# Weight bits on three engines, a softmax in pieces, and a new instruction list, in one fused attention and feed-forward kernel

## The chip, the cores and the metric

The kernel runs on one core of a Trainium2 chip. The core has TensorE (PE in the rows), VectorE (DVE), ScalarE (ACT), GpSimd (POOL) and SyncE (SP), which here only issues DMA transfers. The metric is the device time of one execution in microseconds, from a median of runs.

## What is computed

For 8 batches and 8 heads of 576 rows with 64 columns, linear attention: a softmax of each row of q over its 64 columns, a softmax of each column of k over its 576 rows, a 64 by 64 product of k and v per head, and q times it. The result, 4608 rows of 512, goes through a feed-forward block:

```python
h = x @ w_in                                   # 512 -> 1024
e = np.exp(h - h.max(-1)); sm = e / (e.sum(-1) + 1e-9)
solu = h * sm
ln = (solu - mean(solu)) / sqrt(var(solu) + 1e-6) * g_ln
out = ln @ w_out                               # 1024 -> 512
```

q, k and v are 32-bit floats. The two weights arrive as 64-bit floats, which the kernel turns into 32-bit floats itself.

## The kernel before

The 4608 rows are cut into 36 row tiles of 128. Batches have four whole tiles (c = 0 to 3); the last 64 rows of two neighbouring batches share a fifth. The first four tiles, all of batch 0, are "whole" tiles: they use 32-bit matmuls with unscaled weights. All others use products of 16-bit high and low halves.

Every piece of work is a generator, and one `next` on it is a step. The order is written out by hand: `ORDER` is one string, whose words name the generator to step next, "Q0a.v" meaning that the steps' free operations go to VectorE (".v"), ScalarE (".a") or GpSimd (".p"). Each engine executes its instructions in the order in which the list issues them, so a late instruction holds up all behind it on its engine.

The names in the list: LQb, LKb, LG and the first steps of w, y and V issue loads. Qba, Qbb, Qbc are the softmaxes of q (Q0a and Q0b one whole tile each, Q0c two). Kb is the key side of batch b: the maximum of each column over rows (lines 372 to 377, VectorE), which goes through TensorE to be spread (turned, L348; col, L351; cols, L354; wide, L358; kb, L361), the subtraction (L383, GpSimd or VectorE), exp (L385, ScalarE), 144 small matmuls in two halves (L397), the division (kvn, L409), the largest entry (mx, L413; L172, L175) and from it a power of two s with which the 16-bit copies bd are made (L426 to L432). xt is the attention product of tile t: L561 and two copies xT for whole tiles (the projection after it takes both), L585 with high and low halves (L595, L597) for the others. ht is the first projection of tile t (L612 in four quarters of four matmuls for whole tiles, L620 for others) and the chain behind it (L627 to L676): maximum, exp, a few 128x1 operations for a power of two p, product, sum, high and low halves u, transposing DMA, sum of squares. ot is the second projection (L694) and its eviction. `h` in PSUM has two buffers, so ht starts when the tile two before has had its squares read (L663).

wi and yi (i = 0 to 3) bring 1024 columns' worth of 64-bit words of w_in and w_out into one of two buffers, and `float_of` (L251) makes 32-bit floats of them: ScalarE takes the high words through a scaled Prelu (L259), VectorE shifts the result left by 3 (L261) and ors the top 3 bits of the low words into it (L263). Then ScalarE sums the absolute values (L276, L313). W and Z find the largest sum, a power of two from it, and write the 16-bit high (L288, L335, ScalarE) and low parts (L290, L337, VectorE) of the weights. The 32-bit weights also serve L612 as they are.

P is a group of four matmuls on zeros whose result nobody reads (L751); the list has eight of these. V copies (L212) put v beside a column of ones, on ScalarE unless the list says otherwise.

Of the kernel before, what the change touches and what calls it, by code (L numbers as in the profile page):

```python
# [12 lines left out]
I32 = mybir.dt.int32  # L13
AF = mybir.ActivationFunctionType
# [86 lines left out]
def linear_attention_solu_ffn(ctx: ExitStack, tc: tile.TileContext, q, k, v, w_in, w_out, g_ln, out):  # L101
# [52 lines left out]
    def on(default):  # L154

        return chosen["engine"] or default

    def cast(eng, out, x):
        if eng is nc.scalar:
            eng.copy(out, x)  # L160
# [655 lines left out]
```

## Time and profile before

| | |
|---|---|
| median of 3 runs | 464.75 us (463.77 to 465.03) |
| the profiled execution's own time | 464.6 us |
| its span, first to last instruction | 462.8 us |
| PE busy | 439.2 us, 95% |
| DVE busy | 339.3 us, 73% |
| ACT busy | 285.2 us, 62% |
| POOL busy | 202.6 us, 44% |

The profiled execution lasted 1.8 us longer than its span, and 0.15 us less than the median. In a timeline row the first two numbers are start and duration in microseconds; an instruction that starts behind another on its engine can overlap it by some tenths. Brackets give the engine's idle time before the row and what ended it. A row with "xN" is N instructions in a row, taken together.

### The profile page before, as it was taken

The page shows a single profiled execution, that of the slowest core. Times are in us where ns is not written, and L with a number is a line of the kernel's source. Part 1 is how long each engine was busy: PE and PEld are TensorE (multiplying, and loading weights), DVE is VectorE, ACT ScalarE, POOL GpSimd, SP SyncE. Part 2 cuts the span into 40 slices and gives each one's busy share as a digit, 9 for nine tenths or more (in the row PEclk, how much of TensorE's full clock was granted, in tenths as well). Part 3 has the DMA queues.
Part 4 walks back from the last instruction along what each step waited for, and adds up shares of the span by engine and source line. Part 5 has one row for each costly group of instructions (what it writes and reads, how often), then busy time and mean ns, then how long its engine had stood idle before and what let it go on. Part 6 is the DMA issues. An engine that isn't in the chain of part 4 may idle for free.

```text
span 462.8 us, 8794 instructions
## 1 busy us (share of the span) xinstructions
PE 439.2 (95%) x3379; PEld 212.9 (46%) x3379; DVE 339.3 (73%) x622; ACT 285.2 (62%) x492; POOL 202.6 (44%) x308
## 2 busy tenths in 40 slices
PE   0688999999999999999999999999999999999997
PEld 0344444455445445444544445444454444444445
DVE  4989999987987979986987888675778553541711
ACT  2779998777767768385756674567635654441500
POOL 2112856487776664741455575126613421122010
PEclk9999999999999999999999999999999999999999
DMA  8897866788698496958697857774342562322252
GB/s 280 292 305 267 239 137 184 149 226 203 179 230 187 89 243 111 273 114 217 120 252 153 180 121 185 203 166 86 86 93 68 92 130 77 72 66 68 59 120 72
DMA packets 137386, 73.98 MB, mean 160 GB/s; under 512 B 114168, under 2 KB 122624, under 8 KB 137344
## 3 DMA queue, kind: packets, MB, share of 16 engines
q1 hardware_dynamic: 137344, 73.42, 65.1%
q8 instruction: 26, 0.43, 0.4%
q14 instruction: 16, 0.13, 0.1%
HBM read 36.70 MB, written 9.44 MB: 100 GB/s over the span
## 4 chain that ended last, share of the span: by engine, by line
PE 86%; ACT 7%; DVE 3%; DMA 1%; issue 1%; SPq 0%; ACTq 0%
PE o L694 41%; PE h L620 36%; PE kv L397 4%; PE x L585 3%; DMA km<-in_k_dram 1%; ACT gw L259 1%; ACT e L633 1%; PE h L612 1%; ACT km L385 1%; ACT wi L288 1%; ACT junk_out L313 1%; PE warm_up L751 1%; PE wide L358 1%; DVE iw L263 1%; ACT e L663 1%
## 5 line engine op out<-in xcount | busy, mean ns | idle before, releaser
L694 PE MATMUL o<-wo,uT 128*128 128x512 f16 (+1 forms) x888 | 197.8, 373 | 0.0
L620 PE MATMUL h<-wi,xT 128*128 128x512 f16 x768 | 178.0, 379 | 0.3 <-ACT e L663 0.3
L694 PEld LDWEIGHTS <-uT 128*128 128x128 f16 x888 | 85.8, 98 | 97.7 <-issue 1.6
L620 PEld LDWEIGHTS <-xT 128*128 128x128 f16 x768 | 74.3, 98 | 88.2 <-issue 1.8
L627 DVE TENSOR_REDUCE top<-h 128x1 f32<-128x1024 f32 x36 | 44.0, 1221 | 29.3 <-PE h L620 29.1
L656 DVE SCALAR_TENSOR_TENSOR u<-h,nmu,u 128x1024 f16<-128x1024 f32 x36 | 45.8, 1275 | 16.3 <-ACT u L654 16.1
L663 ACT ACTIVATE e<-h,nmu 128x1024 f32<-128x1024 f32 x36 | 40.1, 1113 | 21.2 <-DVE u L656 21.1
L649 DVE SCALAR_TENSOR_TENSOR h<-h,ph,e 128x1024 f32<-128x1024 f32 x36 | 46.1, 1283 | 8.1 <-POOL ph L646 6.1
L637 POOL TENSOR_SCALAR am<-nm 128x1 f32<-128x1 f32 x20 | 9.1, 454 | 80.7 <-ACT nm L629 80.6
L643 POOL TENSOR_TENSOR p<-pi,mone 128x1 f32<-128x1 f32 x36 | 25.5, 708 | 39.9 <-DVE pi L640 38.4
L654 ACT ACTIVATE u<-h,nmu 128x1024 f16<-128x1024 f32 x36 | 40.0, 1113 | 1.0
L633 ACT ACTIVATE e<-h,nm,hs 128x1024 f32<-128x1024 f32 x28 | 33.7, 1202 | 0.7
L704 ACT ACTIVATE os<-o,rr 128x512 f32<-128x512 f32 (+1 forms) x21 | 14.2, 674 | 30.2 <-PE o L694 22.9
L651 ACT ACTIVATE nmu<-s 128x1 f32<-128x1 f32 x36 | 7.3, 202 | 39.8 <-DVE h L649 31.9
L449 POOL TENSOR_TENSOR qm<-qm,qnmx 128x1024 f32<-128x1024 f32 (+1 forms) x12 | 21.1, 1770 | 20.6 <-DVE qnmx L447 20.5
L612 PE MATMUL h<-iw,xT 128*128 128x512 f32 x64 | 29.5, 599 | 0.1
L629 ACT ACTIVATE nm<-top,hs 128x1 f32<-128x1 f32 x28 | 8.2, 294 | 33.4 <-DVE top L627 33.4
L467 POOL TENSOR_TENSOR qm<-qm,qrec 128x1024 f32<-128x1024 f32 x12 | 23.0, 1920 | 11.7 <-DVE qrec L458 5.4
L383 POOL TENSOR_TENSOR km<-km,kb 128x1152 f32<-128x1152 f32 x10 | 26.3, 2632 | 3.4 <-ACT kb L361 3.2
L597 DVE SCALAR_TENSOR_TENSOR xT<-x,xT 128x512 f16<-128x512 f32 (+1 forms) x36 | 22.3, 623 | 7.2 <-ACT xT L595 7.1
L702 DVE TENSOR_SCALAR os<-o,rr 128x512 f32<-128x512 f32 (+1 forms) x16 | 11.6, 728 | 20.6 <-PE o L694 15.3
L474 POOL TENSOR_TENSOR qhl<-qm,qhl 128x512 f16<-128x512 f32 x20 | 24.1, 1228 | 5.3 <-ACT qhl L160 5.1
(147 smaller groups left out, 559.9 us busy)
## 6 DMA issues: line engine op xcount, KB each, us to landing
v<-in_v_dram SPq DMA_DIRECT2D x32, 288.0 KB, 3.9
km<-in_k_dram SPq DMA_DIRECT2D x7, 1152.0 KB, 6.4
out_dram<-os SPq DMA_DIRECT2D x31, 256.0 KB, 2.7
qm<-in_q_dram SPq DMA_DIRECT2D x7, 1024.0 KB, 6.7
w_in<-in_moe_w_in_dram SPq DMA_DIRECT2D x8, 512.0 KB, 8.4
w_out<-in_moe_w_out_dram SPq DMA_DIRECT2D x8, 512.0 KB, 5.8
out_dram<-os SPq DMA_DIRECT2D x10, 128.0 KB, 2.3
km<-in_k_dram SPq DMA_DIRECT2D x2, 576.0 KB, 6.8
```

Of the source, the lines that this page charges most:

```text
L383: on(nc.gpsimd).tensor_tensor(km[:, ns], km[:, ns], wide, op=ALU.subtract)
L474: on(nc.gpsimd).tensor_tensor(lo, y, hi, op=ALU.subtract)
L612: nc.tensor.matmul(h[:, ns], xT[:, kc], iw[kc][:, ns], start=(i == 0), stop=(i == NP - 1))
L620: nc.tensor.matmul(h[:, ns], xT[:, t, kc], wi[:, s, kc, ns], start=(i == 0), stop=(i == len(terms) - 1))
L627: nc.vector.tensor_reduce(top, h, axis=AX.X, op=ALU.max, negate=True)
L633: nc.scalar.activation(e, h, AF.Exp, bias=nm, scale=hs, accum_out=z)
L643: nc.gpsimd.tensor_tensor(p, pi, mone, op=ALU.pow)
L649: nc.vector.scalar_tensor_tensor(h, h, ph, e, op0=ALU.mult, op1=ALU.mult, accum_out=s1)
L654: nc.scalar.activation(u[:, 0], h, AF.Identity, bias=nmu)
L656: nc.vector.scalar_tensor_tensor(u[:, 1], h, nmu, u[:, 0], op0=ALU.add, op1=ALU.subtract)
L663: nc.scalar.activation(e, h, AF.Square, bias=nmu, accum_out=s2)
L694: nc.tensor.matmul(o, uT[:, j, f], wo[:, s, f, cols], start=(f == 0 and j == 0 and s == 0), stop=(f == NF - 1 and j == 1))
```

## The change

`float_of` takes the bits of the low words in a step of their own ahead of the Prelu, in place in the words' buffer: on GpSimd from the words' top byte (a multiplication and an addition on bytes, rounded to an integer), or on VectorE with a shift where the list says ".v". Left shift and or become one VectorE instruction. The v copies and the high parts of the weights go to ScalarE, or to GpSimd where the list says ".v". In the softmax of q of the four whole tiles, the subtraction, the single exp and the sum on VectorE give way to one exp per head and tile on ScalarE, with the negated maximum as bias and the sum as accumulator output: 8 in Q0a, 8 in Q0b, two steps of 8 in Q0c. `ORDER` is another list of the same steps, 1692 in both.

```diff
@@ v copies
-        cast(on(nc.scalar), vm[:, i, :, 0:D], t)
+        cast(scalar_or_pool(), vm[:, i, :, 0:D], t)
+    def scalar_or_pool():
+        return nc.gpsimd if on(nc.scalar) is nc.vector else nc.scalar
@@ float_of
+        eng = on(nc.gpsimd)
+        if eng is nc.vector:
+            eng.tensor_scalar(low, low, 29, -1, op0=ALU.logical_shift_right, op1=ALU.bitwise_and)
+        else:
+            top = words.bitcast(U8)[:, :, 3]
+            eng.tensor_scalar(low, top, 1.0 / 32, -31.0 / 64, op0=ALU.mult, op1=ALU.add)
+        yield
         nc.scalar.activation(x, high.bitcast(F32), AF.Prelu, scale=2.0**-112, alpha=-(2.0**32))
         yield
-        nc.vector.tensor_scalar(xi, xi, 3, -1, op0=ALU.logical_shift_left, op1=ALU.bitwise_and)
-        yield
-        nc.vector.scalar_tensor_tensor(xi, low, 29, xi, op0=ALU.logical_shift_right, op1=ALU.bitwise_or)
+        nc.vector.scalar_tensor_tensor(xi, xi, 3, low, op0=ALU.logical_shift_left, op1=ALU.bitwise_or)
         yield
@@ weights_in_scaled, weights_out_scaled
-            nc.scalar.activation(wi[:, 0, kc], iw[kc], AF.Copy, scale=s)
+            cast_scaled(scalar_or_pool(), wi[:, 0, kc], iw[kc], s)
-            nc.scalar.activation(wo[:, 0, f], x, AF.Copy, scale=g)
+            cast_scaled(scalar_or_pool(), wo[:, 0, f], x, g)
@@ q_softmax
-        on(nc.gpsimd).tensor_tensor(x, x, wide(nmx), op=ALU.add)
-        yield
-        nc.scalar.activation(x, x, AF.Exp)
-        yield
         sums = sm.tile([P, n], F32, name=f"qsum{name}", tag="qsum")
-        nc.vector.tensor_reduce(shaped(sums), x, axis=AX.X, op=ALU.add)
+        if places is not None:
+            cs = len(places)
+            for c in range(cs):
+                for hd in range(H):
+                    y = x[:, hd] if cs == 1 else x[:, hd, c]
+                    i = slice(hd * cs + c, hd * cs + c + 1)
+                    nc.scalar.activation(y, y, AF.Exp, bias=nmx[:, i], accum_out=sums[:, i])
+                yield
+        else:
...
@@ ORDER, the first words
-    "LQ0*2 LK0 Q0a*2 Q0c LK0 K0.v Q0c.v K0 w3 K0.v K0 Q0b Q0a.v w3 K0 V02 Q0a Q0b K0.v Q0a.v Q0c V00 K0.v "
-    "LG w3 K0.v V02 Q0b.v w0 LG w0 K0 V01 K0.v w3 V00 V03 Q0a w3 K0.v Q0a w2 P w0 w2 K0.v K0 K0.v V01 "
-    "K0.v w0 V03 w0 w3 K0.v P K0 LG w2 w1 Q0b.v Q0c.v K0 Q0b w2 Q0b.v w1 Q0b P K0 x0.v LK1 w0 K0 Q0c.v K0 "
...
+    "LQ0*2 LK0 LG Q0a LG Q0c Q0a Q0b K0 Q0b.v LK0 K0*2 K0.v P K0 Q0c.v V00 V00.v K0 w3 Q0a.v P Q0b.v K0.v "
+    "K0 Q0a w3 V02 Q0b.v w0 K0 P w3.v*2 K0.v Q0a.v w0 w3.v K0 K0.v Q0b.v V01.v Q0b V02.v LG P Q0a V03 w2 "
+    "V01.v K0.v*2 w0.v w0 K0*2 V03.v w2*2 w0.v Q0c K0 V10 K0.v w2.v Q0c*2 w1 w0 K0 x0 w1.v x0 x0.v LK1 "
...
```

In both lists eight P steps stand. In the list before, all eight come behind K0's first transposes on TensorE, three of them ahead of K1's: one before, one between and one behind the two halves of K0's small matmuls. In the new one two come ahead of K0's first transposes, one between these and the spreading ones, one ahead of K0's small matmuls, none between their halves, and four behind K1's first transposes. Of the eight "low" steps of w and y, those of w3 and w0 are on VectorE and six on GpSimd. Up to the step that starts x4, the v copies on ScalarE go from eight to two (V13, V12) and those on GpSimd from none to six; wi's third high part and four of wo's eight are on GpSimd.

## Rows read from the trace of the kernel before

**Rows 1.** The span in five stretches, cut at TensorE's first instruction, at the end of K1's first transposes, at the end of h3's last matmuls and at TensorE's last instruction: start:end and length, busy time and number of instructions of PE, PE's weight load, DVE, ACT and POOL, granted TensorE clock, DMA share, GB/s.

```profile
0.00:14.30 14.30, 0.01 (x1) 0.04 (x1) 8.00 (x20) 4.87 (x7) 3.78 (x9) 1.00 0.88 306
14.30:38.50 24.20, 21.05 (x230) 12.13 (x231) 21.55 (x43) 19.53 (x32) 2.09 (x2) 1.00 0.87 292
38.50:72.30 33.80, 31.28 (x265) 14.32 (x263) 32.50 (x59) 33.39 (x58) 19.97 (x21) 1.00 0.69 184
72.30:459.50 387.20, 386.90 (x2886) 186.41 (x2885) 277.28 (x503) 226.98 (x398) 176.73 (x276) 1.00 0.63 145
459.50:462.80 3.30, 0.00 (x0) 0.00 (x0) 0.00 (x0) 0.47 (x1) 0.00 (x0) 0.85 0.11 40
```

**Rows 2.** The timeline of TensorE from its first warm-up group to the end of h3.

```profile
17.23 1.91 PE L751 MATMUL warm_up<-bd 128*128 128x512 f16 x4
...
22.38 1.89 PE L751 MATMUL warm_up<-bd 128*128 128x512 f16 x4
24.19 1.58 PE L397 MATMUL kv<-vm,km 64*64 64x65 f32 x72
...
27.15 0.67 PE L561 MATMUL x<-qT,kvn 64*64 64x128 f32 x16
...
29.33 3.70 PE L612 MATMUL h<-iw,xT 128*128 128x512 f32 x8
32.87 0.60 PE L519 MATMUL qt<-ident,qn 128*128 128x128 f32 x4
...
38.17 0.38 PE L348 MATMUL turned<-ident,ktop 128*128 128x128 f32 x2
38.39 1.03 PE L751 MATMUL warm_up<-bd 128*128 128x512 f16 x4
...
70.27 1.98 PE L612 MATMUL h<-iw,xT 128*128 128x512 f32 x4
```

**Rows 3.** ScalarE's instructions by line and shape over the span: count, busy us and mean ns of one, idle time before.

```profile
L451 ACT ACTIVATE qm<-qm 128x1024 f32<-128x1024 f32 x15 | 15.8, 1051 | 1.8 <-DVE qm L449 1.4 <-POOL qm L449 0.4
L629 ACT ACTIVATE nm<-top,hs 128x1 f32<-128x1 f32 x28 | 8.2, 294 | 33.4 <-DVE top L627 33.4
L651 ACT ACTIVATE nmu<-s 128x1 f32<-128x1 f32 x36 | 7.3, 202 | 39.8 <-DVE h L649 31.9 <-DVE p_kv L182 5.5 <-DVE den L404 2.4
L259 ACT ACTIVATE iw<-w_in 128x1024 f32<-128x1024 f32 x4 | 4.6, 1140 | 1.7 <-DMA w_in<-in_moe_w_in_dram 1.7
L451 ACT ACTIVATE qm<-qm 128x512 f32<-128x512 f32 x2 | 1.3, 628 | 5.7 <-POOL qm L449 5.7
```

**Rows 4.** The timeline of ScalarE: K0's spreading, its second exp, and a sum of absolute values with the accumulator read behind it and the instruction that follows.

```profile
15.44 0.40 ACT L160 COPY cols<-col 128x256 f32<-128x256 f32 x1 [0.62 <-DVE col L351]
...
16.62 0.37 ACT L361 COPY kb<-wide 128x256 f32<-128x256 f32 x1 [0.20 <-PE wide L358]
...
20.61 1.17 ACT L385 ACTIVATE km<-km 128x1152 f32<-128x1152 f32 x1
...
32.75 1.06 ACT L276 ACTIVATE junk_in<-iw 128x1024 f32<-128x1024 f32 x1 [1.21 <-DVE iw L263]
33.71 0.19 ACT L276 ACTIVATION_READ_ACCUMULATOR junk_in<-iw 128x1 f32 x1
33.80 0.49 ACT L426 ACTIVATE bd<-kvn,s_kv 64x256 f16<-64x256 f32 x1
```

**Rows 5.** The timeline of VectorE: the first two maxima of q, the column maxima, the largest entry of kvn and the last word step of w_in.

```profile
6.12 1.81 DVE L447 TENSOR_REDUCE qnmx<-qm 128x8 f32<-128x512 f32 x2 [5.12 <-DMA qm<-in_q_dram]
...
14.98 0.42 DVE L351 TENSOR_REDUCE col<-turned 128x4 f32<-128x256 f32 x1 [0.24 <-PE turned L348]
...
28.01 0.41 DVE L413 TENSOR_REDUCE mx<-kvn 128x1 f32<-128x256 f32 x1
...
31.43 1.23 DVE L263 SCALAR_TENSOR_TENSOR iw<-w_in,iw 128x1024 int32<-128x1024 int32 x1
```

**Rows 6.** VectorE's and then GpSimd's instructions in the same form.

```profile
L383 DVE TENSOR_TENSOR km<-km,kb 128x1152 f32<-128x1152 f32 x6 | 8.0, 1351 | 0.7 <-ACT kb L361 0.7
L261 DVE TENSOR_SCALAR gw<-gw 128x1024 int32<-128x1024 int32 x4 | 2.7, 684 | 0.0
...
L449 POOL TENSOR_TENSOR qm<-qm,qnmx 128x1024 f32<-128x1024 f32 x10 | 18.9, 1904 | 11.6 <-DVE qnmx L447 11.5
L464 POOL TENSOR_TENSOR qn<-qm,qrec 128x512 f32<-128x512 f32 x2 | 2.1, 1047 | 12.1 <-DVE qrec L458 9.5 <-PE qt L519 2.5
L143 POOL MEMSET bd<- 128x1024 f16 x1 | 1.0, 952 | 0.3 <-POOLq L800 0.3
```

**Rows 7.** The timelines of VectorE and GpSimd at three places where both are busy: one instruction of each per place.

```profile
26.70 1.39 DVE L261 TENSOR_SCALAR iw<-iw 128x1024 int32<-128x1024 int32 x1
...
26.49 1.05 POOL L464 TENSOR_TENSOR qn<-qm,qrec 128x512 f32<-128x512 f32 x1 [2.52 <-PE qt L519]
...
193.93 2.10 DVE L372 TENSOR_TENSOR khalf<-km 128x1024 f32<-128x1024 f32 x1
...
193.04 1.90 POOL L467 TENSOR_TENSOR qm<-qm,qrec 128x1024 f32<-128x1024 f32 x1 [2.33 <-DVE qrec L458]
...
56.97 1.28 DVE L290 SCALAR_TENSOR_TENSOR wi<-iw,s_in,wi 128x1024 f16<-128x1024 f32 x1
...
57.68 2.72 POOL L474 TENSOR_TENSOR qhl<-qm,qhl 128x512 f16<-128x512 f32 x2 [1.22 <-ACT qhl L160]
```

More of the change, by code (lines that the diff above doesn't have):

```diff
@@ L13 @@
 I32 = mybir.dt.int32
+U8 = mybir.dt.uint8
 AF = mybir.ActivationFunctionType
@@ L448, in q_softmax @@
         yield
-        on(nc.gpsimd).tensor_tensor(x, x, wide(nmx), op=ALU.add)
-        yield
-        nc.scalar.activation(x, x, AF.Exp)
-        yield
         sums = sm.tile([P, n], F32, name=f"qsum{name}", tag="qsum")
-        nc.vector.tensor_reduce(shaped(sums), x, axis=AX.X, op=ALU.add)
+        if places is not None:
[7 more added lines that the diff above has]
+        else:
+            on(nc.gpsimd).tensor_tensor(x, x, wide(nmx), op=ALU.add)
+            yield
+            nc.scalar.activation(x, x, AF.Exp)
+            yield
+            nc.vector.tensor_reduce(shaped(sums), x, axis=AX.X, op=ALU.add)
         den = sm.tile([P, n], F32, name=f"qden{name}", tag="qden")
```

139 rows, old and new, of the table ORDER are left out of this document.

## The prediction

> **What bounds the kernel now.** The windows come first: one row per stretch shows in which stretch TensorE idles, and only there can a change give time, since its work is the same in both lists (eight warm-up groups in either). From 72.3 us to its last instruction TensorE is busy 386.90 of 387.20 us [rows 1]: nothing that another engine does faster there can shorten the run. Behind it lie 3.3 us of last eviction and store, in which ScalarE handles the last piece; the new list gives that piece to VectorE at about the same cost, so I leave it. All else lies ahead of 72.3: 14.3 us without TensorE, 24.2 with 3.15 us idle, 33.8 with 2.52 us idle [rows 1]. In these 72.3 us the warm-up groups are TensorE time as well, and lose nothing if they stand where it would idle.
>
> Next the timelines of the head. Its first half, to K1's transposes at 38.17, is a chain through all engines; VectorE is busy 21.55 of 24.20 us there and ScalarE 19.53 [rows 1, 2]. Its second half is TensorE's own work with few gaps, under a ScalarE and a VectorE that are full (33.39 and 32.50 of 33.80) [rows 1]. The question is by how much earlier the new kernel gets to K1's transposes, and whether the two full engines keep up behind them.
>
> **The change part by part.** First the price of a head's exp. A 128x1 ScalarE instruction with one column as operand takes 0.294 us; from 512 to 1024 columns the exp grows from 0.628 to 1.051 us, 0.83 ns a column [rows 3]. So 64 columns with a column as bias: 0.294 + 63 x 0.00083 = 0.346. Each brings an accumulator read of 0.19. The sum of absolute values shows how the two overlap with what follows: 32.75 to 33.80 is 1.05 us for 1.06 + 0.19, so 0.20 is hidden per pair [rows 4]. A head costs 0.346 + 0.19 - 0.20 = 0.336 us and eight 2.7. From below it can't be under 0.20, an instruction of one column with immediates [rows 3], less some overlap: 0.19 is my lower end. From above, without any overlap, 0.54. I take 0.336, since every pair of the trace overlaps.
>
> *Step 1, K0's spreading.* The first maxima stand at about 6.8 (two of them take 6.12 to 7.93 [rows 5]). ScalarE's queue then holds 24 heads (Q0a, Q0b and Q0c's first tile), 8.1 us, and cols behind them: 14.9. Before, cols ran at 15.44 behind col, which ended at 15.40 [rows 4, 5]. The new list lets VectorE reach col earlier, near 13 us, since a subtraction of 1024, a sum, the division and the placing of Q0a no longer all stand ahead of it; so the heads set this step. It gains 0.5 us.
>
> *Step 2, to the end of K0's matmuls.* ScalarE after cols (0.40): Prelu of w3 (1.05 from start to the next start, its 1.14 less the overlap [rows 3]), kb 0.37: 16.7. VectorE: the joined or 1.15 behind the Prelu to 17.5, one subtraction 1.26 (1.35 less overlap [rows 6]) to 18.8. ScalarE: exp, Prelu of w0, exp, three times 1.06: 21.9. Before, the second exp ended at 21.78 [rows 4]: up to here nothing is won. But then TensorE executed a warm-up group (22.38 to 24.27) and only then the second half of the matmuls, to 25.77 [rows 2]. In the new list no group stands there: 21.9 + 1.4 = 23.3. The gain is 2.5.
>
> *Step 3, to h0.* Before, h0 began at 29.33 [rows 2]. Now kvn stands at 24.3, 0.95 after the matmuls (before, 25.77 to mx at 28.01 held a shift of 1.39 and else kvn's small operations [rows 2, 5, 7]). Q0c's second eight heads follow the second exp on ScalarE: 21.9 + 2.7 = 24.6, and VectorE waits for them in its division (0.45) ahead of mx (0.41 [rows 5]) and of x0's copy (0.42): 25.9. h0 takes w1 in its last quarter, some 5.9 us later, 31.8. By the same walk w1's or is done at about 30.3 (before: 31.43 + 1.23 = 32.66 [rows 5]), so it isn't late. The gain at h0's start is 3.4.
>
> *The charge for GpSimd.* GpSimd did almost nothing from 14.3 to 38.5, 2.09 us [rows 1]; now it has up to five v copies and four low pieces there. Beside GpSimd's work a VectorE shift took 1.39 us where the others take 0.684, and a maximum of two SBUF tensors 2.10 (1.2 is usual), 0.88 longer for about 1 us of overlap [rows 6, 7]. The first low pieces and the two subtractions of K0 will meet v copies. These have one input where the rows' GpSimd instructions have two, so I take half of 0.88 for each subtraction: 0.9 us off the gain. From below it is 0, from above 1.8 there; K1's maxima have some 0.9 us to spare. The Trainium skill (GPSIMD Engine Reference, Key points) has GpSimd share its SBUF interfaces with VectorE and names VectorE instructions in a two-port mode or with two SBUF inputs as those that contend. The trace agrees for the shift and the maximum, and not not for the scalar_tensor_tensor of 56.97 with two SBUF inputs, 1.28 us with 0.57 of it beside GpSimd's work. By the rule all or steps and low parts would stretch too, which is the last rival.
>
> *Step 4, to K1's transposes.* From h0's start TensorE executes h0 (16 matmuls, 7.1 at the 3.70 per eight less overlap), x1 0.6, one tile's transposes 0.6 and wide_in 0.3: 25.9 + 8.6 = 34.5, with the charge 35.4, against 38.17 [rows 2]. Before, a second tile's transposes stood here too. The gain is 2.8.
>
> *Step 5, behind them.* The same TensorE work, but one warm-up group fewer (0.86; four stand here, five did) and four transposes more (0.60): 0.26 gained. I leave the idle time of this stretch at 2.52 us [rows 1]. VectorE's queue to the end of the weights and x4 holds eight shifts (8 x 0.62 us) and the sums and a subtraction of Q0 (2.3 and 1.15) less, two low pieces on its own (1.2 each at worst) and a key subtraction (1.26) more, with smaller moves about 3.8 us less work: as much as the gain asks. ScalarE's has 32 heads (10.8) more, and three exps (2.0), six v copies (3.4), four wo and one wi part (3.5) less: 1.9 more, against 14 us of idle time that it had up to 38.5 [rows 1]; its queue now starts at 6.8 rather than 7.96 and waits less.
>
> The sum: 2.8 + 0.26 = 3.1 us. Against the profiled execution's own 464.6 that is 461.5; the median lies 0.15 higher: 461.7.
>
> **What is open from both sides.** A low piece on GpSimd (bytes in steps of eight, 1024 of them): 0.95 us, a memset of 1024, to 1.90, a two-input instruction of 1024 [rows 6], and conversions that no row shows may take it beyond; I take 1.9. A v copy: 0.53 to 1.18 (the memset and the 1.047 of 512, scaled to 576); 1.1 taken. The low piece on VectorE: 0.68, the shift, to 1.22, the or on the same words [rows 5, 6]; 1.2. With 0.19 a head, cols would wait for col at 13 us (1.8 gained) and Q0c's heads give 1.2 more: 3.0, or 458.7.
>
> **The rivals.** *More is won* (459.4): no stretch beside GpSimd (0.9), and of the 2.52 us of idle time 1.4 goes, since h3's matmuls now wait for less. For it speaks that VectorE has less to do; against, that ScalarE is full in that stretch.
>
> *The head's gain is given back* (464.7, no change): DMA has 0.87 of its time filled up to 38.5 [rows 1], the words of w2 and w1 can't be asked for until a buffer is free, and what comes 3 us sooner must be loaded 3 us sooner. If each word block lands 3 us late, h0's last quarters stand where they stood. Against it: the rate there is 292 GB/s, and reached 306 ahead of it [rows 1].
>
> *Slower by dear heads* (468): if the accumulator read doesn't overlap on such short instructions, a head costs 0.54. Then cols starts at 6.8 + 24 x 0.54 = 19.8, 4.9 later, and Q0c's eight cost another 1.6: 3.1 - 6.5 makes it 3.4 slower. It decides from 3.1 / 32 = 0.10 above my price, 0.43 us a head. Against it speaks every accumulator read in the trace.
>
> *Slower by dear low pieces* (467.3): GpSimd's queue is low w2, a placing, low w1, a v copy, low y0, low y1, and then the power p of h0. At 5 us a piece w1's or is 4 us late and p comes 6.9 us later than by 1.9, and with it h0's chain, whose squares free the buffer that h2 waits for: of the 6.9 some 1.2 are absorbed, and 3.1 - 5.7 makes it 2.6 slower. It decides from about 4.2 us a piece. No row shows a GpSimd instruction on bytes.
>
> *Slower by the shared interface* (473): if every VectorE instruction with two SBUF inputs stretched as the maximum did, eight or steps, three wi and eight wo low parts (8 x 1.22, 3 x 1.28, 8 x 0.72, some 19 us) with GpSimd busy for two thirds of it would come 0.88 us later per us of overlap: 11.4, and 3.1 - 11.4 makes it 8.3 slower. Against it speaks the 1.28 of 56.97 [rows 7]. This is what the Trainium skill's rule comes to in this kernel.
>
> **How the numbers follow.** My forecast, 460.4 to 463.3, holds 0.54; more is won 0.16; given back, 463.4 to 466, 0.15; dear heads 0.06, dear low pieces 0.05, the shared interface 0.04. A difference under 0.3% (1.4 us) can't be told from none here. Faster: 0.54 + 0.16 = 0.70; no change 0.15; slower 0.15. The range, 458.7 (cheap heads) to 465.8, leaves out about 0.05 below and 0.14 above.
>
> **What will show it.** Step 1: cols on ScalarE near 14.9, with 24 pairs at 0.34 us apart ahead of it. Step 2: the second half of K0's matmuls ends near 23.3 to 24.2. Step 3: h0 starts at 25.9 to 26.8. Step 4: K1's transposes at 34.5 to 35.4. Step 5: x4's matmuls end near 68.8 to 69.5, where before this list's same work was done at 72.25, and TensorE has no gap of note from there on. Wrong it would be with heads 0.43 us or more apart, a low piece over 4 us on GpSimd, a VectorE row that is stretched beside GpSimd outside maxima and subtractions, or a gap on TensorE behind 72 us.

## The result and the profile after

The new kernel takes 467.15 us (median of 10 runs, 465.97 to 468.48), the kernel before 464.45 beside it (10 runs, 463.77 to 465.89). The ratio is 1.0059 with an interval of 1.0047 to 1.0072: slower by 0.6%, 2.7 us. The forecast was 461.7, and the range ended at 465.8. The profiled execution took 466.36 with a span of 464.6, 1.8 more than before (464.6 and 462.8).

First the windows, cut at the same events as [rows 1]: TensorE's first instruction (8.6), K1's transposes (36.7), the end of x4's matmuls (72.3), a stretch with waits (77) and TensorE's last instruction; the columns are those of [rows 1].

```profile
0.00:8.60 8.60, 0.00 (x0) 0.01 (x1) 2.61 (x7) 3.29 (x13) 1.57 (x7) 1.00 0.76 258
8.60:36.70 28.10, 20.73 (x230) 10.46 (x231) 23.38 (x44) 24.68 (x80) 11.46 (x10) 1.00 0.88 309
36.70:72.30 35.60, 31.01 (x266) 14.54 (x265) 33.61 (x62) 32.02 (x55) 32.08 (x28) 1.00 0.77 213
72.30:77.00 4.70, 3.93 (x17) 1.55 (x18) 3.25 (x4) 4.67 (x7) 4.70 (x4) 1.00 0.91 196
77.00:461.30 384.30, 383.68 (x2871) 184.68 (x2869) 275.02 (x498) 220.67 (x386) 178.71 (x279) 1.00 0.61 142
```

The stretch behind K1's transposes is the one to look at: TensorE idles 4.59 of 35.60 us (before 2.52 of 33.80), and GpSimd, which had 19.97 us of work there, has 32.08. Behind it TensorE idles 1.39 us where it idled 0.30.

Warm-up groups count as busy, so leads are compared without them. TensorE's warm-up work in the kernel before, and then in the new one (busy time of these instructions alone):

```profile
0.00:38.50 38.50, 4.93 (x13) 1.00 0.87 297
38.50:72.30 33.80, 5.05 (x20) 1.00 0.69 184
```

```profile
0.00:36.70 36.70, 5.79 (x16) 1.00 0.85 297
36.70:72.30 35.60, 4.12 (x16) 1.00 0.77 213
```

Before, 21.06 - 4.93 = 16.13 us of useful work were done by 38.5 [rows 1]; now 20.73 - 5.79 = 14.94 by 36.7. The new list is 1.8 us earlier, but has 1.19 less of useful busy time behind it: four transposes of q (0.60) now stand behind K1's, and the other instructions, the same in number, were busy for less time. With 0.93 less warm-up still to come its lead is 1.5 us. TensorE's idle time up to there says the same: 14.29 + 3.15 = 17.44 before, 8.60 + 7.37 = 15.97 now. Then 4.59 - 2.52 = 2.1 are lost ahead of 72.3 and 1.39 - 0.30 = 1.1 behind: 1.5 - 3.2 = -1.7, the 1.8 of the spans within rounding.

TensorE's timeline shows the places (start, duration, in brackets the idle time before and what ended it; "issue" is time in which the engine waited for nothing that the profile shows):

```profile
20.00 1.28 PE L403 MATMUL kv<-vm,km 64*64 64x65 f32 x72 [1.95 <-ACT km L391]
22.20 1.28 PE L403 MATMUL kv<-vm,km 64*64 64x65 f32 x72 [0.92 <-issue]
...
25.91 3.70 PE L627 MATMUL h<-iw,xT 128*128 128x512 f32 x8
...
32.48 1.99 PE L627 MATMUL h<-iw,xT 128*128 128x512 f32 x4 [0.36 <-DVE iw L269]
...
36.33 0.41 PE L354 MATMUL turned<-ident,ktop 128*128 128x128 f32 x2 [0.56 <-DVE ktop L383]
...
60.25 0.32 PE L176 MATMUL kv<-ident,mx 128*128 128x128 f32 x1 [0.88 <-DVE mx L419]
...
67.64 0.32 PE L176 MATMUL wide_out<-ident,m_out 128*128 128x128 f32 x1 [2.56 <-DVE m_out L329]
...
74.56 0.81 PE L709 MATMUL o<-wo,uT 128*128 128x512 f16 x3 [0.41 <-DVE wo L343]
```

Up to h0 all is as forecast: K0's matmuls end at 23.48, h0 starts at 25.91 [rows 2: 29.33]. K1's transposes come at 36.33 [rows 2: 38.17]. The largest loss is one wait: wide_out, the spreading of w_out's largest entry, waits 2.56 us for VectorE's m_out. So what was VectorE late with?

VectorE and then GpSimd in the new kernel:

```profile
17.40 1.35 DVE L389 TENSOR_TENSOR km<-km,kb 128x1152 f32<-128x1152 f32 x1
...
18.74 1.74 DVE L389 TENSOR_TENSOR km<-km,kb 128x1152 f32<-128x1152 f32 x1
...
21.66 1.23 DVE L269 SCALAR_TENSOR_TENSOR iw<-iw,w_in 128x1024 int32<-128x1024 int32 x1
...
41.62 1.28 DVE L296 SCALAR_TENSOR_TENSOR wi<-iw,s_in,wi 128x1024 f16<-128x1024 f32 x1
...
60.11 2.02 DVE L269 SCALAR_TENSOR_TENSOR gw<-gw,w_out 128x1024 int32<-128x1024 int32 x1
...
62.31 1.92 DVE L296 SCALAR_TENSOR_TENSOR wi<-iw,s_in,wi 128x1024 f16<-128x1024 f32 x1
65.05 0.16 DVE L661 TENSOR_TENSOR ph<-p,one 128x1 f32<-128x1 f32 x1 [0.82 <-POOL p L658]
...
65.58 1.27 DVE L664 SCALAR_TENSOR_TENSOR h<-h,ph,e 128x1024 f32<-128x1024 f32 x1
...
67.43 0.16 DVE L329 TENSOR_REDUCE m_out<-g 128x1 f32<-128x4 f32 x1
```

```profile
14.41 0.68 POOL L166 COPY vm<-v 128x576 f32<-128x576 f32 x1 [0.39 <-DMA v<-in_v_dram]
17.70 3.31 POOL L166 COPY vm<-v 128x576 f32<-128x576 f32 x2 [2.60 <-DMA v<-in_v_dram]
...
30.02 1.16 POOL L265 TENSOR_SCALAR w_in<-w_in 128x1024 int32<-128x1024 uint8 x1 [3.55 <-DMA w_in<-in_moe_w_in_dram]
...
55.41 1.66 POOL L166 COPY vm<-v 128x576 f32<-128x576 f32 x1
57.07 2.86 POOL L172 TENSOR_SCALAR wi<-iw,s_in 128x1024 f16<-128x1024 f32 x1
59.90 3.25 POOL L489 TENSOR_TENSOR qhl<-qm,qhl 128x512 f16<-128x512 f32 x2
63.25 1.11 POOL L685 TENSOR_SCALAR z<-z 128x1 f32<-128x1 f32 x1
64.44 0.57 POOL L658 TENSOR_TENSOR p<-pi,mone 128x1 f32<-128x1 f32 x1
```

GpSimd works without a break from 55.4 until it gives p, the power of two of h2, at 65.0; VectorE has ph (p times a factor), h's product with e and the small operations to m_out queued behind it. The v copy and the high half of wi are the moved parts. These rows are longer than elsewhere: the or 2.02 for 1.22, wi's low half 1.92 for 1.28, the v copy 1.66 for 0.68. The two stretched VectorE rows and its wait for p make 0.80 + 0.64 + 0.82 = 2.26 of the 2.56 us.

### The profile page after: what moved, and what is told of

The parts are those of the page before. It is cut to its first block, busy times and chain, and to the rows that moved or that the text cites. A ratio compares the mean times of both kernels' runs of the same rounds, so it can differ in the third digit from the quotient of the medians.

```text
span 464.6 us, 8867 instructions
## 1 busy us (share of the span) xinstructions
PE 439.4 (95%) x3379; PEld 211.2 (45%) x3379; DVE 338.4 (73%) x614; ACT 285.3 (61%) x538; POOL 228.5 (49%) x325
## 4 chain that ended last, share of the span: by engine, by line
PE 84%; DMA 4%; ACT 4%; POOL 4%; DVE 2%; issue 1%; SPq 0%; DVEq 0%; ACTq 0%; POOLq 0%
PE o L709 40%; PE h L635 36%; PE x L600 3%; DMA w_out<-in_moe_w_out_dram 3%; PE kv L403 3%; ACT qm L462 2%; PE h L627 2%; DMA qm<-in_q_dram 1%; POOL wo L172 1%; POOL qhl L489 1%; POOL wi L172 1%; DVE iw L269 1%; ACT iw L267 0%; ACT km L391 0%; POOL qm L465 0%
## 5 line engine op out<-in xcount | busy, mean ns | idle before, releaser
L664 DVE SCALAR_TENSOR_TENSOR h<-h,ph,e 128x1024 f32<-128x1024 f32 x36 | 46.2, 1283 | 4.6 <-POOL ph L661 3.2
L658 POOL TENSOR_TENSOR p<-pi,mone 128x1 f32<-128x1 f32 x36 | 22.6, 627 | 32.2 <-DVE pi L655 31.1
L652 POOL TENSOR_SCALAR am<-nm 128x1 f32<-128x1 f32 x20 | 12.9, 643 | 47.2 <-ACT nm L644 47.0
L482 POOL TENSOR_TENSOR qm<-qm,qrec 128x1024 f32<-128x1024 f32 x13 | 25.0, 1921 | 16.3 <-DVE qrec L473 6.6
L719 ACT ACTIVATE os<-o,rr 128x512 f32<-128x512 f32 x23 | 15.7, 683 | 26.2 <-PE o L709 21.0
L465 POOL TENSOR_TENSOR qm<-qm,qnmx 128x1024 f32<-128x1024 f32 x12 | 22.8, 1899 | 13.2 <-DVE qnmx L453 13.0
L691 POOL TENSOR_TENSOR r<-var,mhalf 128x1 f32<-128x1 f32 x36 | 21.6, 601 | 15.2 <-DVE var L688 8.3
L717 DVE TENSOR_SCALAR os<-o,rr 128x512 f32<-128x512 f32 (+1 forms) x14 | 9.9, 710 | 23.8 <-PE o L709 23.7
```

The source lines that it names most:

```text
L465: on(nc.gpsimd).tensor_tensor(x, x, wide(nmx), op=ALU.add)
L482: on(nc.gpsimd).tensor_tensor(x, x, wide(rec), op=ALU.mult)
L664: nc.vector.scalar_tensor_tensor(h, h, ph, e, op0=ALU.mult, op1=ALU.mult, accum_out=s1)
```

## The experiments

Theory A: GpSimd's queue between 47 and 75 us, stretched beside VectorE, gives the head's gain back. Against it stood B, that moving the parts is wrong in general or the list itself loses; C, that the heads of the q softmax are dear; D, that TensorE's clock falls in the list's new gaps.

**Parts back to ScalarE.** hi_act, the high halves of wi and wo:

```
-            cast_scaled(scalar_or_pool(), wi[:, 0, kc], iw[kc], s)
+            cast_scaled(nc.scalar, wi[:, 0, kc], iw[kc], s)
-            cast_scaled(scalar_or_pool(), wo[:, 0, f], x, g)
+            cast_scaled(nc.scalar, wo[:, 0, f], x, g)
```

> The new kernel with all high parts of the weights back on ScalarE (one wi and four wo leave GpSimd); v copies and low pieces stay. Theory A, GpSimd's queue from 55 us on sets when TensorE fills up: p of h2, at 64.44 in the new kernel, comes near 61.5 (a piece of 2.86 us leaves the queue ahead of it), x4's matmuls end near 69.5 instead of 72.3, the two gaps of o0 behind GpSimd's wo parts go, and the time falls by 2 to 3.5 us to about 464. Theory B, the new list is worse in itself: no change, within 1 us of 467.2. Theory C, the heads on ScalarE are the price: ScalarE gets 4 us more and the time rises by 1 or more.

Measured: 466.14, ratio 1.0039 (1.0022 to 1.0056), 1.0 less than the new kernel; the intervals overlap, and the 2 to 3.5 us of A didn't come. The trace shows where they went; TensorE, and then VectorE:

```profile
49.81 7.13 PE L627 MATMUL h<-iw,xT 128*128 128x512 f32 x16 [1.49 <-ACT e L678]
...
63.91 3.70 PE L627 MATMUL h<-iw,xT 128*128 128x512 f32 x8 [0.99 <-ACT e L678]
67.44 0.29 PE L176 MATMUL wide_out<-ident,m_out 128*128 128x128 f32 x1
```

```profile
61.59 1.22 DVE L269 SCALAR_TENSOR_TENSOR gw<-gw,w_out 128x1024 int32<-128x1024 int32 x1
...
62.99 1.27 DVE L296 SCALAR_TENSOR_TENSOR wi<-iw,s_in,wi 128x1024 f16<-128x1024 f32 x1
64.19 0.15 DVE L661 TENSOR_TENSOR ph<-p,one 128x1 f32<-128x1 f32 x1
```

Without the high half on GpSimd the or and the low half take their usual time, ph no longer waits for p, and the wait ahead of wide_out is gone. In its place TensorE waits 0.99 us for the squares of h1, which now wait for that high half on ScalarE. The 1.49 us belong to words of w_out that landed late in this execution (ScalarE's Prelu at 40.61 waits 1.18 us for them; in the new kernel it stands at 39.21); hi_p below has 0.98 us of the one wait and nothing of the other.

v_act, all v copies instead:

```
-        cast(scalar_or_pool(), vm[:, i, :, 0:D], t)
+        cast(nc.scalar, vm[:, i, :, 0:D], t)
```

> The new kernel with every v copy on ScalarE. Theory A: GpSimd loses a copy of 1.66 us ahead of p of h2 and earlier ones of 0.66 to 1.7 us; p comes 1 to 1.6 us earlier, the time falls by 0.5 to 1.5 us, less than with the high parts. Theory C (ScalarE is the bound because of the heads): six copies of 0.57 us more on it before x4, the time rises by 1 to 3 us. Theory B: within 1 us.

Measured: 471.19, 1.0134 (1.0102 to 1.0167): A's gain didn't come, and the loss is larger than C's. Both edits together, hi_v_act:

> The new kernel with high parts and v copies on ScalarE; only the low pieces stay on GpSimd. Theory A: the two gains add, 3 to 4.5 us off, near 463, and then ScalarE or VectorE is what x4 waits for. Theory C: 5 to 7 us more on ScalarE before x4, slower than the new kernel. Theory B: within 1 us of 467.2.

Measured: 470.93, 1.0149 (1.0115 to 1.0183); here too A's forecast failed. The v copies on GpSimd are worth their place: in v_act's trace K0's small matmuls start at 21.55 instead of 20.00, behind ScalarE, and K1's transposes at 39.66 instead of 36.33, a part of it by a clock of 0.50 from 24 to 32 us. Whether the high halves are can't be told from these runs.

**The heads.** old_q takes back the q softmax alone, in the steps of the new list:

```
-                    nc.scalar.activation(y, y, AF.Exp, bias=nmx[:, i], accum_out=sums[:, i])
+                    on(nc.gpsimd).tensor_tensor(x, x, wide(nmx), op=ALU.add)
+                    nc.scalar.activation(x, x, AF.Exp)
+            nc.vector.tensor_reduce(shaped(sums), x, axis=AX.X, op=ALU.add)
```

> The new kernel with the softmax of q of the first four tiles as before (one subtraction, one exp, one sum, put into the steps of the new list). Theory C: ScalarE has 8.8 us less, the time falls by 2 us or more. Theory A: the head up to K1's transposes moves by at most 1 us either way, and GpSimd's queue behind it still sets the end: the time stays within 1 us of 467.2. Theory B: the same.

Measured: 469.04, 1.0098 (1.0075 to 1.0120): without them the kernel is 1.9 us slower, where A had at most 1 us. The heads gain, and C falls.

**The list alone**, with every part undone (list_only; the q softmax as in old_q, low bits, v copies and high halves as before):

> The new list with every part of the change undone (low bits, shift and or as before in the three steps, v copies on VectorE where the list says so, high parts on ScalarE, q's softmax by one exp). Theory E, the list is what loses: about 467 or more. Theory A: the list fits the parts and is worse without them, since VectorE gets eight shifts, sums and v copies back: 469 to 474. If the list is good and the parts lose: below 464.

Measured: 484.13, 1.0428 (1.0402 to 1.0454), above A's 469 to 474; the theory that the list itself loses (B, called E here) had 467 or more. The list fits its parts and nothing else; this says little of either.

**Low pieces on GpSimd alone**, in the kernel and list before: all eight (low_all), and the four of w_in (low_w).

```
+        top = words.bitcast(U8)[:, :, 3]
+        nc.gpsimd.tensor_scalar(low, top, 1.0 / 32, -31.0 / 64, op0=ALU.mult, op1=ALU.add)
...
-        nc.vector.tensor_scalar(xi, xi, 3, -1, op0=ALU.logical_shift_left, op1=ALU.bitwise_and)
...
-        nc.vector.scalar_tensor_tensor(xi, low, 29, xi, op0=ALU.logical_shift_right, op1=ALU.bitwise_or)
+        nc.vector.scalar_tensor_tensor(xi, xi, 3, low, op0=ALU.logical_shift_left, op1=ALU.bitwise_or)
```

> The kernel before, its own list, with the low bits of all eight word blocks on GpSimd beside the Prelu and one joined shift-and-or on VectorE; nothing else. VectorE loses eight shifts of 0.68 us ahead of 65 us. If VectorE's work bound the head: 1 to 3 us faster, about 462. If GpSimd's queue is the narrow place behind K1: y3's and y2's pieces wait for their words there and hold up K1's second subtraction behind them, 0 to 4 us slower than before.

> The same for the four word blocks of w_in alone, which GpSimd does before 38 us, where it is idle in the kernel before. If VectorE bounds the way to K1's transposes: those come 1 to 2 us earlier and the time falls by 0.5 to 2 us, to about 463. If ScalarE or DMA bounds it: within 0.5 us of the kernel before.

Measured: 465.78, 1.0027 (1.0017 to 1.0037), and 465.14, 1.0019 (1.0007 to 1.0030), though VectorE has eight or four shifts less; neither forecast for low_w came out. low_w shows the stretch by itself; VectorE and then GpSimd:

```profile
13.69 1.16 DVE L386 TENSOR_TENSOR ktop<-khalf 128x128 f32<-128x128 f32 x1
14.89 0.29 DVE L387 TENSOR_TENSOR ktop<-ktop,km 128x128 f32<-128x128 f32 x1
```

```profile
13.60 1.11 POOL L262 TENSOR_SCALAR w_in<-w_in 128x1024 int32<-128x1024 uint8 x1
```

A maximum of 128 columns starts 0.09 us behind GpSimd's piece and ends 0.14 us behind its end; the next one of the same size takes 0.29. It stands ahead of K0's transposes, so TensorE starts at 15.32 where it started at 14.3 [rows 1]. But K1's transposes stand at 38.04 all the same (38.17 before [rows 2]), so this late start isn't what makes low_w 0.8 us slower; that stays open.

**Two steps put back.** w_late leaves all other parts of the change in place. It only moves the third block of wi (high half on GpSimd, low half on VectorE, 57 to 64 us) behind wo's last low half, the high half to ScalarE:

```
-K1 h1 W.v V23.v Q1a P ... h1 K1 W.v y1 ... Z W V23 o0 Z.v x4 h5
+K1 h1 V23.v Q1a P ... h1 K1 y1 ... Z W V23 o0 Z.v W*2 x4 h5
```

> Edit: in the new list the two steps of the third block of wi (high half on GpSimd, then low half on VectorE), which stood at 57-64 us, go to behind the last low half of wo, and the high half goes to ScalarE. Theory A (GpSimd's queue between 47 and 75 us, stretched beside VectorE, gives the head's gain back): wide_out's transposes come 2 to 3 us earlier, at 64.5-65.5 us in place of 67.6, x4 ends at 69-70 in place of 72.3, and the time falls by 2 to 2.6 us to 464.5-465.2. Theory D (TensorE's clock alone, fallen in the gaps before the first tile's product): the gaps at 18-24 us are untouched, so the time stays at 467. If h5 at 76 us now waits for the moved halves, 1 to 2 us are given back there and the time is 466-467 with wide_out early.

Measured: 464.99, 1.0014 (0.9997 to 1.0030): 2.1 of the 2.7 us are back. TensorE:

```profile
64.89 0.32 PE L175 MATMUL wide_out<-ident,m_out 128*128 128x128 f32 x1
65.05 3.60 PE L626 MATMUL h<-iw,xT 128*128 128x512 f32 x8
68.57 0.97 PE L599 MATMUL x<-qT,bd 128*64 128x256 f16 x16
...
71.81 0.81 PE L708 MATMUL o<-wo,uT 128*128 128x512 f16 x3 [0.41 <-DVE wo L342]
...
79.37 2.33 PE L634 MATMUL h<-wi,xT 128*128 128x512 f16 x10 [0.71 <-DVE xT L611]
```

The wait ahead of wide_out is gone, x4 ends 2.8 us sooner, and VectorE's or of y2 takes 1.22 in place of 2.02 (start 60.08). This is what A said, in place and in size. w_late also takes the low half, 1.92 us, off VectorE's queue; hi_act, which leaves it there, shows that the wait ahead of wide_out goes with the high half alone. So GpSimd's queue, with what it does to VectorE beside it, is shown as the cause of that wait. Small waits follow: for wo's low halves, for which VectorE itself waits 1.48 us on GpSimd's high halves, and for xT. wo_late puts wo's high halves on ScalarE as well:

> w_late with the high halves of wo on ScalarE too, no more warm-up groups. Theory A: wo's wait on GpSimd goes (the gap of 0.41 us ahead of o0's third part): 0.4 to 0.8 us below w_late. If ScalarE is late by then: the same as w_late or above it.

Measured: 465.03, 1.0018 (1.0007 to 1.0030): nothing more, where A had 0.4 to 0.8 us.

**The clock.** The 28 runs of the kernel before that stand beside w_late have a mean granted clock of 0.999 or 1.0. The ten of the new kernel have 0.984 to 1.0; its profiled one is at 1.0. wo_late's profiled run is a low one (0.992); its windows, with TensorE's busy time and then the granted clock:

```profile
16.00:20.00 4.00, 1.61 (x11) 1.00 0.65 193
20.00:24.00 4.00, 3.09 (x140) 0.77 0.71 256
24.00:28.00 4.00, 2.99 (x34) 0.50 0.79 230
```

After the gap of 1.95 us ahead of K0's matmuls the clock falls, to half (1.2 GHz) at 24 to 28; h0's first half then takes 4.56 us in place of 3.70. In the profiled executions of the new kernel and of w_late the same gap leaves the clock at 1.00. p_more is the new kernel with six more warm-up groups, four in the gaps at 18 to 24 us and two ahead of wide_out:

```
-w0 K0*2 V03.v ... Q0c K0 V10 ... K1 Z K1 Z.v*2 h0
+w0 K0 P*2 K0 V03.v ... Q0c P K0 P V10 ... K1 Z K1 P*2 Z.v*2 h0
```

> The new kernel with six warm-up groups more, put where TensorE idles: two ahead of K0's small matmuls, one between their halves, one behind them, two ahead of W_out's spreading matmul. Theory D, part of the loss is TensorE's clock, granted at 1.2 GHz for a part of h0 in most executions because the new list leaves TensorE idle ahead of it: the granted clock stays at 1.00 in all executions, and the time falls by 0.5 to 1.5 us to about 466. Theory A (GpSimd's queue from 55 us on) alone: no gain beyond what the clock gives, x4's matmuls still end near 72. If the clock is no cause: the time rises by up to 1 us, since a group takes 0.9 to 1.9 us.

Measured: 466.24, 1.0033 (1.0010 to 1.0057), with the clock at 0.999 or 1.0 in five of its nine runs, 0.993 or more in all. The same six groups in w_late (w_late_p), in hi_act (hi_p), and in wo_late (wo_act_late_p):

> The edit of w_late together with the six more warm-up groups in TensorE's gaps at 18-24 us and ahead of wide_out. Theories A and D together: both gains add, 2 to 2.6 us from GpSimd's queue and 0.8 from the clock, 463.5-464.2, and the runs lie closer together than those of the new kernel. A alone: as w_late. D alone: 466.2, as the warm-up groups alone gave.

> All high halves of wi and wo on ScalarE, with the six more warm-up groups. In the kernel with the high halves alone moved (466.1) TensorE's clock had fallen to half over the first tile's product (4.8 us for one half of it in place of 3.7). Theories A and D together: this goes, 464.8-465.5. If A is wrong and the groups alone matter: 466.2, as with the groups alone. If ScalarE as the new late engine matters most (its squares and exps for the first tiles wait): 466 or more.

> As w_late_p, and the high halves of wo on ScalarE as well; v copies, low pieces and q softmax as in the new kernel. Theory A: the wait for wo's high half at 72-75 us (0.4 and 0.3 us on TensorE) goes also, 0.5 us below w_late_p: 463.0-463.7. If ScalarE is by then the late engine (exps of h, squares): no better than w_late_p.

Measured: 466.25 (1.0018 to 1.0052), 466.16 (1.0026 to 1.0057) and 465.77 (1.0004 to 1.0039): no better than without them, w_late_p 1.3 worse. wide_out comes at 67.20 there: the two last groups, some 0.95 us each, stand where no gap is left. So these were left out (w_late_hp, wo_late_hp: the first two edits of the three).

> The edit of w_late with four of the six more warm-up groups, those in the gaps at 18-24 us; the two ahead of wide_out are left out, since in w_late_p they stood where no gap was left (two groups of about 0.95 us, and wide_out at 67.2 in place of 64.9). Theory A and D: the clock stays at full speed in all runs as in w_late_p, and the 1.9 us of those two groups go: 464.3 or just under it (w_late_p less 1.9), a few tenths below w_late. If the fallen clock costs nothing that other waits would not: as w_late or 0.3 above it, by the 0.3 us that the groups push the first tile's product back (wide_in at 35.8 in place of 35.5).

> wo_late with the four groups in the gaps at 18-24 us. Theories A and D: 1.9 us below the kernel with six groups (465.8), 463.7-464.0, below the kernel before by 0.1 to 0.2 %, with the clock at 1.0 in all runs. If the clock costs nothing: as wo_late or 0.3 above it.

Measured: 466.35 (ratio 1.0028 to 1.0058) and 465.61 (1.0018 to 1.0043), the clock at 1.0 in each run of the first: D, as a way to get the time back, misses. In w_late_hp wide_out stands at 64.78 as in w_late, and the loss comes later, with 0.32 us for a transposed q at 93.6 and 0.56 of "issue" at 227.

**The words of w_in.** SyncE's queue before, and then in the new kernel, shows when the last block's words were asked for:

```profile
17.30 5.25 SPq L248 DMA_DIRECT2D w_in<-in_moe_w_in_dram  x4
```

```profile
17.51 0.80 SPq L252 DMA_DIRECT2D w_in<-in_moe_w_in_dram  x2
19.31 0.33 SPq L214 DMA_DIRECT2D v<-in_v_dram  x1
22.92 1.49 SPq L252 DMA_DIRECT2D w_in<-in_moe_w_in_dram  x2
```

22.92 is where VectorE's or of w0 ends (21.66 + 1.23): the load waits for a buffer. words3_u10 is w_late with a third buffer for words, u10 the same without it; both have two buffers fewer for the float weights and u.

```
-    UB, XB, WB = BUFS
+    UB, XB, WB = BUFS[0] - 2, BUFS[1], BUFS[2] + 1
```

> w_late with a third buffer for the words of a weight block; to make room, two of the twelve buffers that hold the float weights and then the tiles' u go. In the new kernel the last two words loads of w_in are issued at 22.92 us, when VectorE's or of w0 (21.66, 1.23 long) has read its words, and land at 30.0; before they were issued by 22.55 at the latest. If that buffer makes step 4 late: the load is issued some 3 to 5 us sooner, the low piece of w1 begins by 27, TensorE's wait for w1's or in the first tile goes, and K1's transposes come 0.8 to 1.5 us earlier, at 34.8-35.5 in place of 36.3. If DMA as a whole sets it (0.88 of its time filled up to 36.7 us), the load lands at 29 to 30 as before. Whole time against u10, which has the two buffers less and no third one: 0.5 to 1.5 us shorter by the first, the same by the second.

> Control for words3_u10: w_late with ten in place of twelve buffers for the float weights and the tiles' u, nothing else. If the two buffers matter to nobody: w_late's 465.0. If later tiles wait for them: above that, by what words3_u10 then has to be measured against; K1's transposes at 36.3 in either case, since the buffers are not yet all in use there.

Measured: 464.46 (0.9989 to 1.0030) and 464.92 (0.9998 to 1.0039). The load goes out at 19.75 in place of 22.91, and GpSimd's piece no longer waits for data, but starts at 28.18, not by 27 (28.38 in u10). K1's transposes stand at 35.60, 0.7 sooner than in the new kernel and 1.2 sooner than in u10, whose profiled run had h0 at the low clock. But one execution says little here: in the eleven profiled kernels with this head (some with more groups) and no third buffer the load goes out at 22.9 to 23.0, and yet the piece starts anywhere from 28.38 to 30.66 and K1's transposes come at 34.83 to 37.62. That the buffer made step 4 late is thus not shown, and in whole time 0.46 us can't be told from none. In these two kernels the five runs with a clock of 0.999 or 1.0 took 462.3 to 463.8, the others 464.3 to 466.9. words3_p2 therefore fills the one long gap alone (`w0 K0*2` becomes `w0 K0 P*2 K0`).

> words3_u10 with two more warm-up groups in the one gap of 1.95 us ahead of K0's first matmuls (they would end at about 20.1, where those start at 20.07). Theory D: the clock does not fall in most runs; words3_u10's two runs with the clock at 0.999 took 462.3 and 462.7, so the median comes to 462.5-463.5, below the kernel before by 0.2 to 0.4 %. If the groups cost later what they save here, as in w_late_hp, whose clock held in every run and which took 466.35: 464.5 or more.

Measured: 464.61 beside 464.90 for the kernel before, 1.0001 (0.9987 to 1.0014), the clock at 1.0 in 11 of 12 runs. No version beats the kernel before by a difference that can be told. Within these kernels the runs at a low clock are mostly the longer ones, yet kernels that hold the clock are not shorter. Here too, the profile has the wait at 93.4 (0.41) and "issue" at 227 (0.81). The wait stands only in the three kernels with groups in the early gaps and none ahead of wide_out. The "issue" isn't the price of more groups: the new kernel has 0.53 us of it at 228.95 and hi_act 0.50 at 229.72. What both are stays open.

## Why the prediction was wrong

- **Heads and steps 1 to 3: right.** Activation and accumulator read repeat every 0.33 us (0.336 predicted), cols ran at 14.76 (14.9), K0's matmuls ended at 23.48 (23.3 to 24.2), h0 began at 25.91 (25.9 to 26.8). These are the lower ends, without the charge. "Dear heads" falls.
- **Low pieces: too dear in the sum.** 1.11 to 1.19 us each on GpSimd, once 1.50, where 1.9 was taken. "Dear low pieces" falls, and that its 467.3 lies beside the measured 467.15 is chance. Its mechanism, a power p that waits in GpSimd's queue, did come, but for h2 and behind other parts.
- **Step 4: 1 to 2 us too early.** The step that failed is "By the same walk w1's or is done at about 30.3 ... so it isn't late". It ended at 31.20 + 1.22 = 32.42, hardly before the old 32.66: its words were asked for only at 22.92, when a buffer came free, and GpSimd's piece began at 30.02. That is the mechanism of "the head's gain is given back", for one block; how much of the lateness is the buffer and how much the landing isn't shown. K1's transposes came 1.8 us sooner where 2.8 was forecast, and with what the new order puts off the lead was 1.5 us, not 3.1.
- **The charge for GpSimd and the shared interface: the reading of one row failed.** I took 0.9 us for two subtractions (1.35 and 1.74 us, so 0.4) and nothing for or steps and low parts, because the scalar_tensor_tensor of 56.97 wasn't stretched [rows 7]. But that one started first, 0.71 us ahead of GpSimd's instruction, so it wasn't the one to wait. Where VectorE came second its or steps and low parts waited as well: 1.69 and 2.02, 1.81 and 1.92 us. The Trainium skill (SBUF — State Buffer, Who interferes with whom) has the pair of ports as an exclusive lock that goes to whichever starts first, for its whole instruction, if VectorE's has two inputs in SBUF and GpSimd's reads SBUF. The trace agrees, with low_w's 1.16 us. The rival's sum of 11.4 us was far too large all the same: up to 72.3 us the or steps and wi's low parts are stretched by 2.6 us in all, since only those that come second pay.
- **Step 5: the term "I leave the idle time of this stretch at 2.52 us" failed**; it was 4.59, 2.56 of it ahead of wide_out. GpSimd's queue wasn't followed there: a high half of 2.86 us and a v copy of 1.66, on top of its own work there, kept it full from 55.4 to 65.0, and the short p of h2 stood behind them. w_late and hi_act show it. Nor is there "no gap of note" behind x4: 1.1 us more than before, with 0.41 and 0.29 for wo's low halves and 0.53 of "issue" at 229. Steps 4 and 5 together, 1.6 us of lead and 3.2 of idle time, are the 4.8 us between the 461.5 forecast for the profiled execution and its 466.36.
- **"Lose nothing if they stand where it would idle"** left out that the groups also hold the clock: w_late's runs have 0.989 to 1.0, those of w_late_p and w_late_hp 0.999 or 1.0. The old list had one ahead of, between and behind the halves of K0's small matmuls; the new one leaves 1.95 us empty ahead of them. Of the 2.7 us between the medians the profiled runs show 1.8. The other 0.9 fits the lower clock of most runs, but the groups that hold it gave no time back, so this share isn't shown.

## What to carry to other kernels

Work moved to an idle engine is priced with that engine's queue where it lands: ask which tiny step on the path stands behind it. Where a VectorE instruction with two inputs in SBUF met a GpSimd instruction here, the one that came second was longer by about the rest of the other; look at start times before a row is taken as proof of no contention. And a lead of one engine's events is no lead in work: subtract what the new order puts off, and the warm-up.

## What was not expected of the hardware

The wait went both ways: GpSimd's copy of 128x576 took 0.68 us alone and 1.66 behind VectorE's or of 55.21. VectorE's product with e (L664), which reads h from PSUM and e from SBUF, took 1.27 at 65.58 though GpSimd's subtraction of 1.90 had started at 65.47, and a reduction at 56.47 kept its 1.21 beside GpSimd's copy.
